# GpSimd's share of a sine in a top-k attention and cosine-gate kernel: reduced early in a slot only, with other chunk counts and another warm-up

## The chip, the cores and the metric

The kernel runs on one core of one Trainium2 chip. The metric is the device time of one execution in microseconds (us). Four executions of the kernel before took 1465.86, 1465.92, 1466.25 and 1466.51 us; their median is 1466.09 us.

## The reference

Inputs are `q`, `k`, `v` of shape (8, 8, 576, 64), `w_in` of shape (512, 2048) and `w_out` of shape (2048, 512). Cut to what matters:

```
scores = (1/8) * q @ k^T                       # per batch and head, 576 x 576
kth    = 32nd largest value of each row
attn   = softmax(where(scores >= kth, scores, -1e9))
x      = (attn @ v), heads side by side        # 4608 tokens x 512
h      = x @ w_in                              # 4608 x 2048
out    = (h * cos(h)) @ w_out                  # 4608 x 512
```

The weights arrive as 64-bit floats, and the kernel makes 32-bit ones of them itself ("decoding").

## The kernel before

**Units and slots.** A unit is 128 rows of queries (tokens) by one pair of heads. There are 36 blocks of 128 tokens and four pairs of heads, so 144 units; four units make a block of `x`. The program is one loop over slots, written out by hand, and the scheduler keeps that order on each engine: slot i looks for the top 32 values of unit i on VectorE, makes the exponentials of unit i-1 on ScalarE, sends unit i-2 out for its transpose, and in every even slot multiplies units i-4 and i-3 with `v` on TensorE. In this document slot i begins with VectorE's instruction at L255 (`rest`), the first of its search.

**One unit on its way.** TensorE makes the scores (L228) into two PSUM tiles, `sc` for columns 0 to 447 and a strip of `rim` for the rest. ScalarE copies them to SBUF (`take_scores`: L240 and L243; for unit 0 alone in three pieces, L242, L243, L245). VectorE folds the two halves of each row (L255, maximum), GpSimd adds and subtracts to get the minimum (L273, L282; in slots 7 to 11 VectorE takes the minimum itself, L263), and VectorE searches four times eight maxima in `rest` and two times eight in `low` (L360, L365). ScalarE masks (L389, L391) and exponentiates (L399). GpSimd splits the words into 16-bit halves (L432, L434), SyncE writes them to DRAM (`rows`, L442) and reads them back by a transposing DMA (`pT`, L448). TensorE multiplies with `v` (L485) into `rim`, and VectorE scales the result into `xT` (L494). As the values stand in the same bank as the strip of scores, ScalarE's L243 of an even slot comes behind L485, and L494 behind that.

**The second layer.** When all four units of a block are in `xT`, TensorE computes `h` in eight steps (`ff1`, L545), two of them to one of two PSUM banks `mm`, four of them to one tile `g` of 1024 columns. ScalarE empties a bank in two instructions (`take_first`, L559 and L561: a scaled copy `g` and a rounded copy `x`). Then GpSimd forms the argument of the sine, `g` minus the rounded number (`reduce_first` L581, `reduce_second` L590), ScalarE computes the sine (`sines`, L600, with a table load before it and another before the next L399), GpSimd multiplies (`gate`, L607), and TensorE computes `o` in eight steps of two columns of `w_out` each (`ff2`, L620). ScalarE empties `o` (L630) and writes it out. `feed` hands TensorE such steps at three places in each slot, and decides while the program is built, by counters: a tile that was reduced in a slot gets its sine in a later one, and `ff2` may use a gated tile two calls of `feed` after its gate (three in later slots). `w_out` may be used once `wq["ready"]` counts it.

**Weights.** 32 chunks of 512 KB, 16 of `w_in` and then 16 of `w_out`, are loaded by `load_weights(n, queue)` (L122) at the start of the slots: three before slot 0, then `n` in each slot, on SyncE's queue in slots 0 and 1 and on ScalarE's own queue after that. A chunk is decoded by ScalarE at the end of its slot (`decode_first`, L135 and L138), by VectorE after the third search of the next slot (L146) and by GpSimd right behind (L156), the chunk that came last first. A staging tile is shared with the tiles `g`, seven in all, and a load that finds none is left to the next slot.

**The order in a slot** of what the change touches:

```
load_weights(n, nc.sync if i < 2 else nc.scalar)
if x: send(x)
topk_first(u, w); fold_low(u); topk_round(u, 1); topk_round(u, 2)
decode_second(NP); decode_third()
...
feed(1); scores; values; sines; mask; take_banks(); exponentials; take_scores
topk_round(u, 3, both(w), z)
gate(1); feed(2); take_banks(); decode_first(NP)
reduce_first(); reduce_second()
feed(3)
```

Before the loop TensorE runs seven multiplications of a tile of ones (L813), the two head pairs of the first block are asked for, and unit 0's scores are made and taken.

Of the kernel before, what the change touches and what calls it, by code (L numbers as in the profile page):

```python
# [10 lines left out]
F32 = mybir.dt.float32  # L11
# [6 lines left out]
P = 128  # L18
# [12 lines left out]
def kernel(  # L31
# [9 lines left out]
    nc = tc.nc  # L41
# [6 lines left out]
    NP = H // 2  # L48
    NF = DF // P
    HS = S // 2  # L50
# [7 lines left out]
    small = ctx.enter_context(tc.tile_pool(name="small", bufs=4))  # L58
# [2 lines left out]
    ffw = ctx.enter_context(tc.tile_pool(name="ffw", bufs=2))  # L61

    ident = consts.tile([P, P], F32, tag="ident")
    ones = small.tile([P, P], F32, tag="ones", name="ones", bufs=1)
    nc.vector.memset(ones, 1.0)
    make_identity(nc, ident)
    halfpi = consts.tile([P, 1], F32, tag="halfpi")
    nc.vector.memset(halfpi, math.pi / 2.0)
# [26 lines left out]
        chunks.append((moe_w_out[f * P : (f + 1) * P, :], w))  # L95
    CHUNKS, XB = 7, 4
    BUSY = range(7, 12)
    ff = {"live": 0, "tick": 0, "now": 0, "credit": 0.0, "end": False, "kind": 0, "half": 0, "open": 0}

    wq = {"next": 0, "loaded": deque(), "second": deque(), "third": deque(), "done": 0, "ready": 0}  # L100

# [49 lines left out]
    def decode_third():  # L151

        while wq["third"]:
            st, w, _ = wq["third"].pop()
            wi = w.bitcast(I32)
            nc.gpsimd.tensor_tensor(out=wi, in0=wi, in1=st[:, :, 0], op=ALU.add)  # L156
            wq["done"] += 1
# [58 lines left out]
    SB = 448  # L216
# [18 lines left out]

    def take_scores(u):
        s = u["s"] = work.tile([P, 2, S], F32, tag="s", name="s", bufs=4)
        head = u["n"] == 0
        if not head:
            nc.scalar.copy(out=s[:, :, 0:SB], in_=u["sc"][:, :, 0:SB])  # L240
        else:
            nc.scalar.copy(out=s[:, :, HS:SB], in_=u["sc"][:, :, HS:SB])  # L242
        nc.scalar.copy(out=s[:, :, SB:S], in_=sc_ends[u["n"] % 2])  # L243
        if head:
            nc.scalar.copy(out=s[:, :, 0:HS], in_=u["sc"][:, :, 0:HS])  # L245
        if not u["folds"]:
            del u["sc"]

# [51 lines left out]
    def topk_first(u, w):  # L300

        u["top"] = tops[u["n"] % len(tops)]
        merges = w and w["folds"]
        if merges:
            merge_first(w)
        if u["folds"]:
            if u["n"] not in BUSY:
                fold_sum(u)
            fold_high(u)
        else:  # L310
            u["rest"] = work.tile([P, 2, S], F32, tag="rest", name="rest", bufs=1)
        if merges:
            merge_second(w)
        if u["folds"] and u["n"] in BUSY:
            fold_now(u)
        topk_round(u, 0, [lambda: bounds(w), lambda: distances(w)] if w else ())

    def topk_round(u, rnd, between=(), ahead=None):
        top, rest, lasts = u["top"], u["rest"], TOPK // 8 - 1
        end = TOPK - 1 - 8 * rnd  # L320
        at = top[:, :, end : end - 8 if rnd < lasts else None : -1, 0]
        if u["folds"]:
            search(
                at, rest[:, :, HS:S] if rnd == 0 else rest[:, :, 0:HS], rest[:, :, 0:HS], rnd < lasts,
                between if rnd < lasts else (),
            )
        else:
            search(at, u["s"] if rnd == 0 else rest, rest, rnd < lasts, between)
        if rnd < lasts:
            return  # L330
        del u["rest"]
        if u["folds"]:
            low = u.pop("low")
            for k in range(TOPK // 16):
                more = k < TOPK // 16 - 1
                if ahead and not more:
                    take_values(ahead)
                search(
                    top[:, :, 1 + 8 * k : 9 + 8 * k, 1], low, low, more,
                    () if more or rnd < lasts else between,  # L340
                )
# [3 lines left out]
    def merge_first(u):  # L345
        n = TOPK // 2 + 1
        u["lesser"] = u["top"].rearrange("p j r i -> p j (r i)")[:, :, 2 * n : 3 * n]
        nc.vector.tensor_reduce(
            out=u["lesser"], in_=u["top"][:, :, 0:n], axis=mybir.AxisListType.X, op=ALU.min
        )  # L350

    def merge_second(u):
        nc.vector.tensor_reduce(
            out=u["top"][:, :, TOPK - 1, 1], in_=u.pop("lesser"), axis=mybir.AxisListType.X,
            op=ALU.max,
        )
# [57 lines left out]
    def both(u):  # L414
        return [lambda: sums(u), lambda: reciprocal(u)] if u else ()
# [88 lines left out]
    for w in widths:  # L504
        blk = {"t0": t0, "w": w, "left": 0, "g": [], "gated": []}
# [12 lines left out]
    fresh = deque()  # L518
# [38 lines left out]
    def take_first(blk, g, x, mm, half):  # L557
        at = slice(half * 512, half * 512 + 512)
        nc.scalar.mul(out=g[:, at], in_=mm, mul=INV_2PI / UP)  # L559

        nc.scalar.activation(  # L561
            out=x[:, at].bitcast(I32), in_=mm, func=AF.Identity, bias=quarter, scale=INV_2PI / UP
        )
        if half == 1:
            fresh.append([blk, g, x, False])

    def take_banks():
        while full:
# [2 lines left out]

    def reduce_first():

        if not fresh:
            return
        _, g, x, _ = fresh[0]
        fresh[0][3] = True
        if ff["end"]:
            nc.vector.tensor_tensor(out=x, in0=g, in1=x.bitcast(I32), op=ALU.subtract)
            return  # L580
        nc.gpsimd.tensor_scalar(  # L581
            out=x, in0=x.bitcast(I32), scalar1=1.0, scalar2=0.0, op0=ALU.mult, op1=ALU.add
        )

    def reduce_second():
        if not fresh or not fresh[0][3]:
            return
        blk, g, x, _ = fresh.popleft()
        if not ff["end"]:
            nc.gpsimd.tensor_tensor(out=x, in0=g, in1=x, op=ALU.subtract)  # L590
        waiting.append((blk, g, x, ff["now"]))
# [104 lines left out]
    for n in range(NP, len(order)):  # L696
        i = last[order[n - 5]] if n >= 5 else 0
        load_at(max(i, 2 * NP + 2), load_qk, *order[n])
        i = last_values[order[n - 6]] if n >= 6 else 0
# [13 lines left out]
    def send(x):  # L713

        split(x)
        write_halves(x)
        transposes(x)

    def slot(i, u, w, x, z):
        n = 4 if i in (1, 2) else 3 if i < NP else 2  # L720
        if i < NP:
            for load, b, hp in at_once[i]:
                load(b, hp)
        load_weights(n, nc.sync if i < 2 else nc.scalar)
        if x:
            send(x)
        topk_first(u, w)
        fold_low(u)
        topk_round(u, 1)
        topk_round(u, 2)  # L730
        decode_second(NP)
        decode_third()
        made = scored.get(i, [])
        if z:
            take_banks()
        feed(1)

        for m in made:
            scores(m)
        if z:  # L740
            values(z)


        late = len(made) > 0

        decoding = i < 3 * NP
        if i % 2 or decoding:
            sines(1)
        if w:
            mask(w)  # L750
        take_banks()
        if w and late:
            exponentials(w)
        take_scores(units[i + 1])
        if w and not late:
            exponentials(w)
        topk_round(u, 3, both(w), z)
        if i in at_slot:
            load, b, hp = at_slot[i]
            load(b, hp)  # L760
        gate(1)
        feed(1 if len(made) == 2 else 2)
        take_banks()
        decode_first(NP)
        reduce_first()
        reduce_second()
        feed(1 if len(made) == 2 else 3)
        if i == LAST:
            sines(1)

    def last_slot(i, u, w, x, z):
        if u:
            topk_first(u, w)
            fold_low(u)
            topk_round(u, 1)
        else:
            bounds(w)
            distances(w)
        mask(w)
        exponentials(w)  # L780
        take_banks()
        sines(1)
        if z:
            values(z)
        if i + 1 < NU:
            scores(units[i + 1])
        if z:
            take_values(z)
        if i + 1 < NU:
            take_scores(units[i + 1])  # L790
        if x:
            send(x)
        if u:
            topk_round(u, 2, both(w))
            topk_round(u, 3)
        else:
            sums(w)
            reciprocal(w)
        normalise(w)
        gate(2)  # L800
        feed(2)
        transposes_now(w)
        take_banks()
        reduce_first()
        reduce_second()
        feed(1)
        values([w])
        take_values([w])
        feed(2)

    tt = ps.tile([P, 512], F32, tag="mm", name="warm", bufs=2)
    for _ in range(7):
        nc.tensor.matmul(tt[:, 0:P], ones, ones, start=True, stop=True)  # L813
    load_qk(0, 0)
    load_qk(0, 1)
    load_weights(3, nc.sync)
# [3 lines left out]
    for i in range(NU + 1):  # L820
# [4 lines left out]
        u, w = (units[i - n] if 0 <= i - n < NU else None for n in range(2))  # L825
        x = units[i - 2] if 0 <= i - 2 < LAST else None
# [52 lines left out]
```

## Time and profile before

| | |
|---|---|
| median of four executions | 1466.09 us |
| the profiled execution's own time | 1466.51 us |
| its span | 1464.7 us |
| mean granted clock of TensorE | 0.973 |
| busy: TensorE, VectorE, GpSimd, ScalarE | 1388.1, 1362.9, 1157.0, 1088.7 us |
| instructions | 30242 |

The span is the time from the first to the last instruction of the profiled execution, 1.8 us less than the execution's own time. A matrix multiplication of 32-bit floats leaves two records on TensorE, a transpose one. The profile's chain of waits follows the work that ended last back to the start; a line of the timeline shows start, busy time, engine, line and operands, and in brackets the idle time before it and what ended that.

### The profile page before, as it was taken

How to read it: one execution, taken by the hardware profiler on the slowest of the kernel's cores; microseconds unless marked ns; L12 is line 12 of the kernel's file. 1: busy time of each engine (PE TensorE's matmuls, PEld its weight loads, DVE VectorE, ACT ScalarE, POOL GpSimd, SP SyncE). 2: the span in 40 equal slices, each digit the busy share in tenths (PEclk: the TensorE clock that was granted, in tenths of full speed). 3: DMA queues.
4: the chain of work that ended last, by engine and by line, in shares of the span. 5: the costliest groups of instructions: out<-in, count | busy, mean ns of one | idle time of the engine just before them, and what ended most of it. 6: DMA issues, size and time to landing. Idle time of an engine off the chain costs nothing.

```text
span 1464.7 us, 30242 instructions
## 1 busy us (share of the span) xinstructions
PE 1388.1 (95%) x10290; PEld 1000.1 (68%) x10290; DVE 1362.9 (93%) x5214; ACT 1088.7 (74%) x1911; POOL 1157.0 (79%) x812
## 2 busy tenths in 40 slices
PE   4378899999999999999999999999999999999998
PEld 2165667777777777777777766777777776777675
DVE  7999899999999999999999999999999999999821
ACT  5777677777777777777777777777777777777641
POOL 5876788888888887888888888888888888888410
PEclk6589999999999999999999999999999999999999
DMA  8977576666665666657655666667665576655200
GB/s 264 278 216 206 151 187 173 159 168 175 192 151 152 152 197 171 166 152 187 190 159 149 151 183 180 170 148 183 192 173 144 144 176 167 163 148 151 62 8 15
DMA packets 427434, 240.00 MB, mean 164 GB/s; under 512 B 375952, under 2 KB 392592, under 8 KB 427280
## 3 DMA queue, kind: packets, MB, share of 16 engines
q1 hardware_dynamic: 418704, 216.88, 56.5%
q10 hardware_dynamic: 8576, 21.19, 4.3%
q8 instruction: 81, 1.33, 0.4%
q14 instruction: 73, 0.60, 0.1%
HBM read 45.09 MB, written 101.19 MB: 100 GB/s over the span
## 4 chain that ended last, share of the span: by engine, by line
PE 86%; DVE 5%; ACT 4%; DMA 3%; POOL 1%; issue 1%; SPq 0%; ACTq 0%; POOLq 0%
PE mm L545 33%; PE o L620 33%; PE rim L485 11%; PE sc L228 8%; DVE top L360 2%; PE rim L228 2%; DVE rest L365 1%; DMA st<-in_moe_w_in_dram 1%; ACT s L399 1%; ACT s L391 1%; DMA v<-in_v_dram 1%; DMA rows<-halves 1%; DMA pT<-rows 0%; ACT x L561 0%; ACT L600 0%
## 5 line engine op out<-in xcount | busy, mean ns | idle before, releaser
L545 PEld LDWEIGHTS mm<-xT,w_in 128*128 128x128 f32 x4608 | 541.4, 193 | 77.9 <-issue 64.6
L545 PE MATMUL mm<-xT,w_in 128*128 128x128 f32 x4608 | 544.8, 277 | 10.8 <-DVE xT L494 7.9
L620 PE MATMUL o<-w_out,g 128*128 128x512 f32 x1152 | 538.4, 601 | 8.6 <-POOL g L607 7.4
L360 DVE MAX8 top<-rest 128x8 f32<-128x288 f32 x1148 | 480.7, 454 | 0.0
L432 POOL COPY halves<-s 128x2304 uint16<-128x2304 uint16 x140 | 294.6, 2104 | 151.0 <-ACT s L399 149.7
L365 DVE MATCH_REPLACE8 rest<-top,rest 128x288 f32<-128x288 f32 (+1 forms) x860 | 377.1, 446 | 0.0
L620 PEld LDWEIGHTS o<-w_out,g 128*128 128x128 f32 x1152 | 203.0, 191 | 197.3 <-issue 186.5
L360 DVE MAX8 top<-low 128x8 f32<-128x288 f32 x568 | 239.9, 448 | 2.7 <-POOL low L282 2.7
L399 ACT ACTIVATE s<-s,nd 128x576 f32<-128x576 f32 x288 | 220.2, 767 | 0.8
L391 ACT ACTIVATE s<-s,top 128x576 f32<-128x576 f32 x288 | 206.1, 766 | 0.0
L282 POOL TENSOR_TENSOR low<-low,rest 128x576 int32<-128x576 int32 x137 | 193.5, 1412 | 10.7
L273 POOL TENSOR_TENSOR low<-s 128x576 int32<-128x576 int32 x137 | 193.4, 1412 | 5.7 <-ACT s L245 4.4
L228 PE MATMUL sc<-k,q 64*128 64x448 f32 (+1 forms) x640 | 154.2, 585 | 35.4 <-DMA k<-in_k_dram 15.0
L559 ACT ACTIVATE g<-mm 128x512 f32<-128x512 f32 x144 | 85.9, 596 | 130.1 <-PE mm L545 125.9
L590 POOL TENSOR_TENSOR x<-g,x 128x1024 f32<-128x1024 f32 x68 | 160.9, 2367 | 5.7
L485 PE MATMUL rim<-pT,v 128*64 128x128 f32 (+1 forms) x2560 | 159.4, 268 | 5.7 <-DMA pT<-rows 5.7
L607 POOL TENSOR_TENSOR g<-g,x 128x1024 f32<-128x1024 f32 x68 | 160.9, 2366 | 1.3 <-ACT x L600 1.3
L485 PEld LDWEIGHTS rim<-pT,v 128*64 128x64 f32 x2560 | 132.6, 139 | 16.0 <-issue 7.0
L240 ACT COPY s<-sc 128x896 f32<-128x896 f32 x143 | 128.4, 898 | 0.7 <-ACT ob L630 0.4
L243 ACT COPY s<-rim 128x256 f32<-128x256 f32 x144 | 55.1, 382 | 94.1 <-PE rim L485 94.1
L365 DVE MATCH_REPLACE8 low<-top,low 128x288 f32<-128x288 f32 x284 | 123.6, 443 | 0.0
L228 PEld LDWEIGHTS sc<-k,q 64*128 64x128 f32 (+1 forms) x640 | 46.4, 181 | 97.0 <-DVE rest L365 49.6
(62 smaller groups left out, 1334.6 us busy)
## 6 DMA issues: line engine op xcount, KB each, us to landing
rows<-halves SPq DMA_DIRECT2D x140, 640.0 KB, 3.0
out_dram<-ob ACTq DMA_DIRECT2D x36, 256.0 KB, 2.3
q<-in_q_dram SPq DMA_DIRECT2D x31, 288.0 KB, 3.6
v<-in_v_dram SPq DMA_DIRECT2D x32, 256.0 KB, 3.3
st<-in_moe_w_out_dram ACTq DMA_DIRECT2D x16, 512.0 KB, 4.5
st<-in_moe_w_in_dram SPq DMA_DIRECT2D x10, 512.0 KB, 6.6
k<-in_k_dram SPq DMA_DIRECT2D x31, 144.0 KB, 3.6
k<-in_k_dram SPq DMA_DIRECT2D x32, 128.0 KB, 3.6
```

The costliest lines, as they stand in the source:

```text
L228: nc.tensor.matmul(to[r0 : r0 + rows, j, 0 : k1 - k0], st["q"][d, q0 : q0 + rows], st["k"][d, k0:k1], start=True, stop=True,)
L273: nc.gpsimd.tensor_tensor(out=u["low"].bitcast(I32), in0=s[:, :, 0:HS], in1=s[:, :, HS:S], op=ALU.add)
L282: nc.gpsimd.tensor_tensor(out=low, in0=low, in1=u["rest"][:, :, HS:S].bitcast(I32), op=ALU.subtract)
L360: nc.vector.max(to[:, j], src[:, j])
L365: nc.vector.match_replace(rest[:, j], to[:, j], src[:, j], NEG)
L391: nc.scalar.activation(out=s[:, j], in_=s[:, j], func=AF.Prelu, bias=less[:, j, 1:2], scale=1.0, alpha=FAR)
L399: nc.scalar.activation(out=s[:, j], in_=s[:, j], func=AF.Exp, bias=nd[:, j : j + 1], scale=SCALE, accum_out=den[:, j, 0:1],)
L432: nc.gpsimd.tensor_copy(out=halves[:, :, 0 : 2 * S], in_=s.rearrange("p (k h) -> p h k", h=2))
L485: nc.tensor.matmul(o[d, to], lhsT, rhs, start=c == 0, stop=c == NT)
L545: nc.tensor.matmul(mm[:, at : at + w], w_in[f // FC][:, c, (f % FC) * P : (f % FC + 1) * P], blk["xT"][:, c], start=c == 0, stop=c == NC - 1,)
L590: nc.gpsimd.tensor_tensor(out=x, in0=g, in1=x, op=ALU.subtract)
L620: nc.tensor.matmul(o, g[:, at : at + P], w_out[f], start=f == 0, stop=f == NF - 1)
```

## The change

Four edits:

1. `reduce_first` and `reduce_second` are called at a second place too, right behind `decode_third()`. A new flag `ff["late"]` is set behind the fourth search of a slot and cleared at the start of the next. A tile whose second bank is emptied while the flag is set carries the number of that slot, and `reduce_first` leaves it until the next slot.
2. The chunk counts `n` of slots 0, 1, 2, ... were 3, 4, 4, 3, 2, 2, 2, ...; they are 3, 4, 3, 2, 2, 2, 2, 2, 3, 3, 3.
3. `take_scores` of unit 0 copies in two pieces as for every other unit.
4. The seven multiplications of a tile of ones, which VectorE had filled, become twelve transposes of the identity, which GpSimd makes; the tile of ones is gone.

```
-    ones = small.tile([P, P], F32, tag="ones", name="ones", bufs=1)
-    nc.vector.memset(ones, 1.0)
...
     def take_scores(u):
         s = u["s"] = work.tile([P, 2, S], F32, tag="s", name="s", bufs=4)
-        head = u["n"] == 0
-        if not head:
-            nc.scalar.copy(out=s[:, :, 0:SB], in_=u["sc"][:, :, 0:SB])
-        else:
-            nc.scalar.copy(out=s[:, :, HS:SB], in_=u["sc"][:, :, HS:SB])
+        nc.scalar.copy(out=s[:, :, 0:SB], in_=u["sc"][:, :, 0:SB])
         nc.scalar.copy(out=s[:, :, SB:S], in_=sc_ends[u["n"] % 2])
-        if head:
-            nc.scalar.copy(out=s[:, :, 0:HS], in_=u["sc"][:, :, 0:HS])
...
         if half == 1:
-            fresh.append([blk, g, x, False])
+            fresh.append([blk, g, x, False, ff["now"] if ff["late"] else 0])
...
     def reduce_first():
-        if not fresh:
+        if not fresh or (ff["late"] and not ff["end"] and fresh[0][4] == ff["now"]):
             return
...
     def slot(i, u, w, x, z):
-        n = 4 if i in (1, 2) else 3 if i < NP else 2
+        n = (3, 4, 3, 2)[i] if i < NP else 2 if i < 2 * NP else 3
...
+        ff["late"] = False
         topk_first(u, w)
         fold_low(u)
         topk_round(u, 1)
         topk_round(u, 2)
         decode_second(NP)
         decode_third()
+        reduce_first()
+        reduce_second()
...
         topk_round(u, 3, both(w), z)
+        ff["late"] = True
...
-    for _ in range(7):
-        nc.tensor.matmul(tt[:, 0:P], ones, ones, start=True, stop=True)
+    for _ in range(12):
+        nc.tensor.transpose(tt[:, 0:P], ident, ident)
```

`last_slot`, which runs for the last three units and the slot behind them, clears the flag at its start and reduces where it did.

More of the change, by code (lines that the diff above doesn't have):

```diff
@@ L97 @@
     BUSY = range(7, 12)
-    ff = {"live": 0, "tick": 0, "now": 0, "credit": 0.0, "end": False, "kind": 0, "half": 0, "open": 0}
+    ff = {"live": 0, "tick": 0, "now": 0, "credit": 0.0, "end": False, "kind": 0, "half": 0, "open": 0, "late": False}
     wq = {"next": 0, "loaded": deque(), "second": deque(), "third": deque(), "done": 0, "ready": 0}
@@ L572, in reduce_first @@
     def reduce_first():
-        if not fresh:
+        if not fresh or (ff["late"] and not ff["end"] and fresh[0][4] == ff["now"]):
             return
-        _, g, x, _ = fresh[0]
+        g, x = fresh[0][1:3]
         fresh[0][3] = True
@@ L587, in reduce_second @@
             return
-        blk, g, x, _ = fresh.popleft()
+        blk, g, x, *_ = fresh.popleft()
         if not ff["end"]:
@@ L771, in last_slot @@
     def last_slot(i, u, w, x, z):
+        ff["late"] = False
         if u:
```

## The prediction

> **What bounds the kernel now.** I read the chain of waits first, then TensorE's waits by stretch, then the timelines of the stretch that was left.
>
> ```profile
> PE 86%; DVE 5%; ACT 4%; DMA 3%; POOL 1%; issue 1%; SPq 0%; ACTq 0%; POOLq 0%
> ```
>
> TensorE (PE) is the chain. Asked for the stretch 185 to 1340 us, its waits are none at all. So the order of the two programs decides what can matter: from slot 16 on, every engine's instructions stand in the same order in both, the last slots too; only the chunk loads and decodings of slots 2 to 11, the order of a few steps of TensorE in slots 9 to 13, five reductions (slots 7, 8, 13 before; 8, 9, 14 after, two of them simply later) and the start differ. The end therefore moves by as much as the last moment at which TensorE still waits, and by what its clock does there. That moment is here:
>
> ```profile
> 166.44 0.61 PE L545 MATMUL mm<-xT,w_in 128*128 128x128 f32 x4
> 171.26 5.02 PE L545 MATMUL mm<-xT,w_in 128*128 128x128 f32 x28 [4.21 <-DVE xT L494]
> ```
>
> The 28 records behind it take 5.02 us where 28 of the usual pace (3.57 for 32) take 3.1: the granted clock there is 0.50 for 172 to 175 us. I call 171.26 the resumption. It is VectorE's xT of slot 14. VectorE's slots begin (L255) at 39.29 (slot 3), 50.47, 64.99, 74.65, 84.70, 95.00 (slot 8), 106.08, 117.84, 128.51, 138.80, 149.14, 160.17 (slot 14). The work is to move these.
>
> **Part 1: fewer early chunks.** The chain in slots 3 and 4:
>
> ```profile
> 45.24 8.12 DMA rows<-halves
> 53.38 7.17 DMA pT<-rows
> ...
> 60.68 1.97 PE L485 MATMUL rim<-pT,v 128*64 128x128 f32 x16 [4.79 <-DMA pT<-rows]
> ...
> 63.53 0.49 DVE L494 TENSOR_TENSOR xT<-rim,pT 128x128 f32<-128x128 f32 x2 [1.79 <-ACT s L243]
> ```
>
> Unit 1's `rows` take 8.12 us where 3.0 is the median, because three chunks were issued at 43.17 to 44.5 and the transposing read of unit 0 took SyncE's queue 7.89 us to issue (35.28 to 43.17), with four chunks in flight. The other such reads took 2.5 us without chunks and 4.4 to 5.1 with two, so about 1.3 per chunk. After: three chunks there, 1.3 off, so `rows` is issued at 43.9; two chunks beside it, so 512 KB less at the 420 GB/s of 48 to 52 us, 1.2 off. It lands at 50.7, 2.6 earlier, and `pT` at 57.9. TensorE then runs its 40 records partly at the full clock that it has at 56 to 59.6 us (1.3 instead of 2.4 us at best), so xT gains 2.7 to 3.8.
>
> Does VectorE get there? In slot 4 its L146 takes 3.00 us for two where 0.36 each is usual, while GpSimd runs L273 and L282 (55.89 to 58.83). GpSimd was held by L432 until the `rows` landed (53.36); now L156 has three chunks instead of four (1.25 less) and it is through at about 56, so L146 is nearly free, and one of three falls away (0.36). Slot 3 also begins 0.3 earlier (ScalarE issues one chunk less, 0.45 us on the chain at 34.66; VectorE was waiting 0.27) and has one L146 less. VectorE could be at L494 at 59.0. **Gain at slot 5: 3.4 us, from 2.4 (only the transfers' 2.6) to 4.5 (VectorE's own bound).** Slots 5 to 7 keep their lengths (9.66, 10.05, 10.30; no waits in them, two chunks as before). The chunks moved to slots 8 to 10 cost VectorE 0.36 in slots 9 and 11 and meet DMA shares of 0.6 to 0.85, so nothing else.
>
> **Part 2: the reductions of the first block.** Before:
>
> ```profile
> 104.65 2.38 POOL L607 TENSOR_TENSOR g<-g,x 128x1024 f32<-128x1024 f32 x1
> 106.98 1.07 POOL L581 TENSOR_SCALAR x<-x 128x1024 f32<-128x1024 int32 x1
> 108.13 2.36 POOL L590 TENSOR_TENSOR x<-g,x 128x1024 f32<-128x1024 f32 x1
> ...
> 113.50 2.54 POOL L156 TENSOR_TENSOR w_out<-w_out,st 128x512 int32<-128x512 int32 x2 [0.41 <-ACT s L391]
> 115.99 2.37 POOL L607 TENSOR_TENSOR g<-g,x 128x1024 f32<-128x1024 f32 x1
> ...
> 107.08 3.65 PE L620 MATMUL o<-w_out,g 128*128 128x512 f32 x4 [3.53 <-POOL g L607]
> ```
>
> The first tile is reduced at the end of slot 7, gets its sine in slot 8, and its gate ends at 107.03, 0.95 into slot 9; TensorE starts `o` then. After, that tile is emptied late in slot 7, so it is reduced in slot 8 behind L156; its sine stands in slot 9 and its gate at the end of slot 9, and on GpSimd's queue that is behind slot 9's three L156 and the second tile's reduction. TensorE's order still has eight columns of `o` (16 records) ahead of the scores of units 11 and 12, which slot 10's copies and values need. Counted from slot 9's L255: L146 at 6.28 (112.36 less 106.08), three in 1.09, 0.13 to GpSimd, three L156 3.7 (15.32 to 19.05), L581 1.13, L590 2.31, L607 2.37, TensorE 0.05 later: 17.1. The 16 records 8.8 (107.08 to 115.89, also from a cold clock), scores and values 4.5 (120.33 to 124.82), L243 and L494 0.5, to the next L255 1.43: slot 11 begins 32.3 after slot 9. Before it was 22.4. **Loss: 9.9 us.** TensorE idles some 19 us ahead of `o` instead of 3.53 and 2.53, and VectorE about 11 ahead of slot 10's L494. Behind the late gate on GpSimd's queue stands unit 8's split (L432), some 5 us later, and behind that its `rows` and `pT` on SyncE's; they are wanted in slot 12 only, 25 us on.
>
> Slot 8 loses its sine and two table loads (1.28 each) on ScalarE, so its L494 no longer waits 0.30: **gain 0.3**.
>
> **Part 3: slots 11 to 14.** Before, from slot 11 to the resumption: 42.75 us. In it VectorE waited 0.53 (slot 12) and 2.71 here, on its `low`:
>
> ```profile
> 160.58 1.04 POOL L581 TENSOR_SCALAR x<-x 128x1024 f32<-128x1024 int32 x1 [3.27 <-ACT x L561]
> ...
> 169.34 0.82 DVE L360 MAX8 top<-low 128x8 f32<-128x288 f32 x2 [2.71 <-POOL low L282]
> ```
>
> GpSimd stood 3.27 us at L581 of a bank emptied late, with the split and slot 14's L273 and L282 behind it. After, that reduction stands behind L282, which ends 2 us before VectorE asks. Slot 11 10.64 (10.29 and an L146), slot 12 9.81, slot 13 11.03 (its wait of 1.93 for the exponentials stays: ScalarE's sine is 1.1 sooner, but one more bank is emptied ahead of them, 1.15), and 8.38 in slot 14: 39.9. **Gain 2.9.** TensorE's own new waits there (GpSimd's L156 ahead of `o` in slot 12, about 2; a bank in slot 13, 2.4) lie under VectorE's slots; without that cover they would cost up to those amounts.
>
> **The clock at the resumption.** TensorE will have stood 1.8 us there instead of 4.21. Stalls of 1.26, 1.33 and 1.83 us (138.98, 157.36, 83.60) left the clock at 1.00, but one of 1.88 (127.41) was followed by 0.50. I take the warm case, 1.9 less 0.5 for unit 13's `pT`, which then comes late in slot 16: **gain 1.4**; the other bound is 0.
>
> The Trainium skill, "TensorE: Matmul & The Clock Gate", Part 1, says that the array goes cold only after about 3.4 us of idleness and warms after as much activity. By it the 1.8 us are safe and the gain is 1.4; the row at 127.41 speaks against it. The same rule speaks against the new warm-up, as twelve records are shorter than a window.
>
> **Part 4: the start**, costed at nothing. The 14 warm records (0.234 apart, from 1.05) become 12 (a transpose leaves one) from about 1.35, when GpSimd's identity is ready: scores of unit 0 at 4.2 instead of 4.33. If they ran at half clock they would take 2.3 (like 51.27 to 53.57) instead of 1.44. The copies are 0.1 shorter (0.79 and 0.37 for 1.25). All of it lies under slot 0's waits for the weights, 0.34 and 1.13 in VectorE's L146 (13.15, 14.71); without these it would cost at most 0.8.
>
> **Sum.** -3.4 - 0.3 + 9.9 - 2.9 - 1.4 = +1.9 us on the profiled execution's 1466.5, so 1468.4; that execution was 0.4 above the median, so 1468.0 us. About 0.2% (2.9 us) is what a measurement can tell from no change here; 1468.0 is inside it, close to its edge at 1469.0.
>
> **Rivals.** (a) Slower: the early relief is small. `rows` of unit 1 stays behind `v`, whose 512-byte pieces share the engines with the chunks, and `pT` still ends last in slot 4. With 1.0 instead of 3.4 the time is 1470.4; it decides below 2.4. For it: the shares of 0.95 and more at 46 to 52 us, which two chunks also fill. Against: the 1.3 us per chunk in the issue times. (b) Slower: slot 9's L146 collide with GpSimd as in slot 4 (2.2 us), or the resumption is cold (1.4): 1469.4 to 1471.6. Against: GpSimd should be free from 4.8 to 7.5 in slot 9. (c) Faster: the pause of Part 2 doesn't come, because I read the order wrong and `o` doesn't need that gate so early; then 9.9 goes and 1458 stays; it decides when TensorE's wait ahead of `o` is under 14 us. With half the pause, 1463.
>
> **How the numbers follow.** Forecast 0.46, (a) 0.24, (b) 0.17, (c) 0.13. Both (a) and (b) end over 1469.0: slower 0.41, same 0.46, faster 0.13. The forecast's own range is 1465 to 1469. The low end of the whole range, 1464.0: relief 4.5 (-1.1), slot 13's wait gone (-1.9), a warmer start of `o` (-1). The high end, 1472.0: relief 1.0 (+2.4) and a cold resumption (+1.4), rounded up.
>
> **What would show it.** Slot 5 begins near 61.6 and `pT` of unit 1 lands near 58; `rows` of unit 1 takes under 7 us; TensorE waits for the gate once, for 17 to 20 us, ending near 119.5; VectorE waits 10 to 12 us at slot 10's L494; no wait on `low` in slot 14; the resumption near 174.6, at full clock; no waits of TensorE from 190 to 1340. I am wrong if the wait for the gate is short, if slot 5 begins after 63, or if TensorE waits anew in the long stretch.

## The result and the profile after

| | before | after |
|---|---|---|
| median, runs | 1466.66 us, 68 | 1469.55 us, 43 |
| ratio of after to before, 95% interval | | 1.0024, 1.0017 to 1.0030 |
| the profiled execution's own time | 1466.51 us | 1467.65 us |
| its span | 1464.7 us | 1465.8 us |

The change makes the kernel 3.5 us slower by the ratio (2.5 to 4.4), 2.9 by the medians. That is just over the 0.2% that the prediction took as the limit of what can be told from no change. The profiled executions differ by 1.1 us only: before's lies at its median, after's 1.9 below its own. One execution each of e1 (1499.30 us) and of e3 (2762.67 us) below fell into a slower state and is left out of their ratios.

Line numbers are those of the kernel that ran. In after and the kernels built on its start they are 2 to 8 lower than in before: L255 is L247 there, L485 is L477, L494 is L486, L607 is L599, L620 is L612, L146 is L144.

The page's chain of waits of after, first line:

```profile
PE 82%; DVE 10%; ACT 4%; DMA 2%; SPq 1%; issue 1%; POOL 1%; ACTq 0%; POOLq 0%
```

VectorE's share has doubled and TensorE's is 4 points lower. TensorE's waits from 185 to 1340 us are 0.4 us in all, so the time is again made before slot 16. In nine profiled executions of kernels with and without parts of the change (before, after, e1 to e4, e9 to e11) the execution's time less the moment at which slot 16 begins lies between 1283.6 and 1285.2 us; in the other four, e5 to e8, which share a chip, between 1282.3 and 1282.5. So what the edits do they do by slot 16, and the 2 us behind it go with the chip.

The early slots of after, in the chain of waits by time (start, duration, what) and in VectorE's timeline:

```profile
42.31 6.60 DMA rows<-halves
48.93 6.46 DMA pT<-rows
...
59.82 0.75 DVE L247 TENSOR_TENSOR rest<-sc,s 128x576 f32<-128x576 f32 x1
```

Unit 1's `rows` take 6.60 us instead of 8.12, its `pT` lands at 55.4 instead of 60.6, and slot 5 begins at 59.82, 5.17 earlier.

The pause, in the timelines of GpSimd and TensorE:

```profile
108.01 3.77 POOL L154 TENSOR_TENSOR w_out<-w_out,st 128x512 int32<-128x512 int32 x3 [2.63 <-issue]
111.74 1.05 POOL L573 TENSOR_SCALAR x<-x 128x1024 f32<-128x1024 int32 x1
112.88 2.38 POOL L582 TENSOR_TENSOR x<-g,x 128x1024 f32<-128x1024 f32 x1
115.20 2.36 POOL L599 TENSOR_TENSOR g<-g,x 128x1024 f32<-128x1024 f32 x1
...
117.62 10.05 PE L612 MATMUL o<-w_out,g 128*128 128x512 f32 x16 [16.60 <-POOL g L599]
```

Slot 9 begins at 100.51, so TensorE starts `o` 17.1 us into it. Slots 9 and 10 take 33.54 us together. In the windows of the same stretch (length, then busy time and instructions of each engine, PEclk, DMA share, GB/s) the clock behind the pause is cold until about 124:

```profile
116.00:120.00 4.00, 2.38 (x3) 1.18 (x4) 4.00 (x18) 3.97 (x6) 3.95 (x3) 0.50 0.41 166
120.00:124.00 4.00, 4.00 (x6) 1.54 (x5) 3.53 (x13) 2.53 (x5) 2.62 (x3) 0.56 0.40 164
124.00:128.00 4.00, 4.00 (x11) 1.63 (x11) 0.00 (x0) 0.00 (x0) 4.00 (x2) 1.00 0.95 193
```

Slots 11 to 14 and the resumption, on TensorE:

```profile
171.76 0.61 PE L537 MATMUL mm<-xT,w_in 128*128 128x128 f32 x4
173.48 3.39 PE L537 MATMUL mm<-xT,w_in 128*128 128x128 f32 x28 [1.11 <-DVE xT L486]
```

The 28 records behind xT run at full clock, 3.39 us instead of 5.02, and VectorE no longer waits for `low`.

### The profile page after: what moved, and what is told of

It reads as the page before. It is cut to its first block, busy times and chain, and to the rows that moved or that the text cites. A ratio compares the mean times of both kernels' runs of the same rounds, so it can differ in the third digit from the quotient of the medians.

```text
span 1465.8 us, 30229 instructions
## 1 busy us (share of the span) xinstructions
PE 1389.2 (95%) x10288; PEld 999.1 (68%) x10288; DVE 1360.3 (93%) x5213; ACT 1088.0 (74%) x1910; POOL 1156.5 (79%) x812
## 4 chain that ended last, share of the span: by engine, by line
PE 82%; DVE 10%; ACT 4%; DMA 2%; SPq 1%; issue 1%; POOL 1%; ACTq 0%; POOLq 0%
PE o L612 31%; PE mm L537 30%; PE rim L477 10%; PE sc L226 7%; DVE top L352 4%; DVE rest L357 3%; PE rim L226 2%; DMA pT<-rows 1%; DMA rows<-halves 1%; DVE rest L247 1%; ACT s L391 1%; ACT L391 1%; DVE low L357 1%; DMA k<-in_k_dram 1%; ACT s L383 0%
## 5 line engine op out<-in xcount | busy, mean ns | idle before, releaser
L612 PE MATMUL o<-w_out,g 128*128 128x512 f32 x1152 | 539.5, 602 | 19.9 <-POOL g L599 16.6
L612 PEld LDWEIGHTS o<-w_out,g 128*128 128x128 f32 x1152 | 203.5, 191 | 209.3 <-issue 187.6
L226 PE MATMUL sc<-k,q 64*128 64x448 f32 (+1 forms) x640 | 157.2, 590 | 34.6 <-DVE rest L247 13.7
L477 PE MATMUL rim<-pT,v 128*64 128x128 f32 (+1 forms) x2560 | 160.4, 270 | 3.1 <-DMA pT<-rows 3.1
L599 POOL TENSOR_TENSOR g<-g,x 128x1024 f32<-128x1024 f32 x68 | 160.8, 2364 | 1.3 <-ACT x L592 1.3
L477 PEld LDWEIGHTS rim<-pT,v 128*64 128x64 f32 x2560 | 133.5, 139 | 13.2 <-issue 3.3
```

Of the source, the lines that this page charges most:

```text
L226: nc.tensor.matmul(to[r0 : r0 + rows, j, 0 : k1 - k0], st["q"][d, q0 : q0 + rows], st["k"][d, k0:k1], start=True, stop=True,)
L477: nc.tensor.matmul(o[d, to], lhsT, rhs, start=c == 0, stop=c == NT)
L612: nc.tensor.matmul(o, g[:, at : at + P], w_out[f], start=f == 0, stop=f == NF - 1)
```

## The experiments

All are compared with the kernel before, run beside them on the same chip; three groups share a chip each: e1 to e4 (before's median 1466.07), e5 to e8 (1468.30), e9 to e11 (1466.00). A comparison of ratios across groups also compares chips; no profile of before was taken beside e5 to e8. The ratio carries an interval of 0.1 to 0.2%; an amount in us is the ratio's distance from 1 times 1466. Single profiled executions scatter by up to some 5 us about their kernel's median, so a profile is used for its waits and the ratio for the time.

| | ratio, 95% interval | median | profiled |
|---|---|---|---|
| e1 chunk counts alone | 1.0019 (1.0004 to 1.0035) | 1469.20 | 1465.45 |
| e2 reductions alone | 1.0017 (1.0007 to 1.0027) | 1469.93 | 1469.03 |
| e3 start alone | 1.0001 (0.9987 to 1.0016) | 1466.10 | 1470.57 |
| e4 after, early reduction from slot 12 on only | 0.9993 (0.9975 to 1.0010) | 1464.87 | 1459.98 |
| e5 = e1 with one chunk moved from slot 10 to slot 7 | 0.9979 (0.9964 to 0.9994) | 1463.47 | 1462.12 |
| e6 = e4 with that chunk moved | 0.9957 (0.9942 to 0.9972) | 1461.95 | 1459.43 |
| e7 after, TensorE kept busy in the pause | 0.9989 (0.9979 to 0.9999) | 1466.48 | 1466.84 |
| e8 after, slot 9's gate ahead of the reduction | 0.9980 (0.9969 to 0.9991) | 1465.36 | 1464.22 |
| e9 after once more | 1.0023 (1.0012 to 1.0033) | 1469.68 | 1467.95 |
| e10 = e7 with more transposes | 1.0036 (1.0017 to 1.0054) | 1471.48 | 1476.56 |
| e11 late reductions alone | 0.9976 (0.9965 to 0.9987) | 1462.48 | 1465.62 |

**e1, the chunk counts alone.**

```
-        n = 4 if i in (1, 2) else 3 if i < NP else 2
+        n = (3, 4, 3, 2)[i] if i < NP else 2 if i < 2 * NP else 3
```

> The kernel before with the second edit alone (the other chunk counts). Theory (the trace of after shows slot 5 beginning 5.2 us earlier than before; fewer chunks beside unit 0's transposing read and unit 1's rows are the cause): slot 5 begins at 60 to 61 us, unit 1's rows take under 7 us, slot 4's two L146 take under 1 us, and the time is 4 to 5.5 us under before, near 1461.5 us, the resumption in slot 14 being earlier by as much. Rival 1 (the relief comes for the most part from the new start, by which the weights' transfers fall otherwise): slot 5 begins after 63 us and the time is within 1.5 us of before. Rival 2 (the chunks that arrive later cost as much in slots 8 to 11): slot 5 near 60 but the resumption unchanged at 171, time within 1.5 us of before.

Slot 5 begins at 59.16, as the theory has it, and still the kernel is 2.8 us slower (0.6 to 5.1). The theory's time fell, and rival 2 is the nearer one, though e1 is worse than it allowed. The profiled execution is 3.8 under its median and no slower than before's, so it can't show the 2.8; it shows where most of the relief goes, on TensorE in slots 8 and 9:

```profile
97.84 1.98 PE L485 MATMUL rim<-pT,v 128*64 128x128 f32 x16 [4.32 <-DMA pT<-rows]
...
115.20 2.08 PE L620 MATMUL o<-w_out,g 128*128 128x512 f32 x2 [5.96 <-POOL w_out L156]
```

The second line is a wait that neither before nor after has in these slots. `o`'s eighth column needs the eighth chunk of `w_out`, which now comes in slot 8 and is decoded by GpSimd in slot 9, behind the second tile's reduction (L156 three times, 111.38 to 115.14). With before's counts it was decoded in slot 8. The first line is unit 5's transposing read, which landed 12.8 us after its issue began, beside three loads; before's took 9.3 beside two. Slots 8 and 9 take 27.34 us instead of before's 22.84, so 4.5 of the 5.8 us by which slot 5 began earlier are gone by slot 10.

**e2, the reductions alone**: before with the first edit, old counts, old start.

```
+        ff["late"] = False
         topk_first(u, w)
...
         decode_third()
+        reduce_first()
+        reduce_second()
...
         topk_round(u, 3, both(w), z)
+        ff["late"] = True
```

> The kernel before with the first edit alone (the reductions). Theory (the gate of the first block's first tile comes a slot later and TensorE stands ahead of o): one wait of TensorE ahead of o of 14 to 18 us in slot 9, slot 9 to slot 11 10 to 11.5 us longer than before's 22.4, slots 11 to 14 shorter by 2 to 3 and the resumption warmer by up to 1.9: time 5 to 8 us over before, 1471 to 1474 us. If slot 9's unpredicted 1 us more (VectorE's wait of 2.97 at L399) is due to the third chunk of that slot, it is absent here, and the pause costs 10. Rival (the whole difference of after comes from elsewhere and the pause is absorbed): within 1.5 us of before.

```profile
119.97 9.96 PE L620 MATMUL o<-w_out,g 128*128 128x512 f32 x16 [18.77 <-POOL g L607]
```

The pause is there: 18.77 us once, slot 9 to slot 11 31.86, slot 14 9.38 instead of 12.20. With two chunks in slot 9 instead of three the gate ends 15.5 us after the slot's start instead of 17.1. The time, 2.5 us over before (1.0 to 4.0), is under the 5 to 8 expected: the mechanism holds and its price at the end is smaller than its price in slots 9 and 10. In the trace these two take 9.4 us more than before's, slots 11 to 15 give 4.6 of it back, and slot 9 had begun 1.6 earlier, so slot 16 begins 3.2 later. Besides, as e3 and e11 below show, executions with before's order have waits of their own in the same place.

**e3, the start alone**: twelve transposes and the uncut copies.

```
-    for _ in range(7):
-        nc.tensor.matmul(tt[:, 0:P], ones, ones, start=True, stop=True)
+    for _ in range(12):
+        nc.tensor.transpose(tt[:, 0:P], ident, ident)
```

> The kernel before with the third and fourth edits alone (the start). Theory (slot 0 begins 0.5 later since the twelve transposes leave the clock cold, all of it under VectorE's waits for the weights): within 0.7 us of before. Rival 1 (the new start moves the weights' transfers so that slot 1 begins 1.2 us earlier, as in the trace of after): 1 to 1.5 us under before. Rival 2 (the cold scores cost their time): 0.5 to 1 us over before.

The ratio is 1.0001: the start costs nothing, as predicted. Its profiled execution shows the scatter: slot 10 takes 13.96 us where before's took 10.67, with the same program there, by

```profile
128.45 1.97 PE L477 MATMUL rim<-pT,v 128*64 128x128 f32 x15 [3.69 <-DMA pT<-rows]
```

The same wait is 2.90 in e11 and 3.67 in e5. Slots 9 and 10 of kernels with before's order and counts there take 22.43 (before), 23.82 (e11) and 25.68 us (e3). Before's one profile, from which the prediction took 22.43, was the shortest of the three.

**e4, without the pause.**

```
-        reduce_first()
-        reduce_second()
+        if i >= 3 * NP:
+            reduce_first()
+            reduce_second()
...
-        ff["late"] = True
+        ff["late"] = i >= 3 * NP
```

> The changed kernel, with the early reduction and the flag from slot 12 on only; up to slot 11 a tile is reduced at the end of a slot as before. Theory (the relief of 5.2 us, the 2.9 us of slots 11 to 14 and the warmer clock add, and the pause is the only loss): no wait of TensorE ahead of o over 5 us in slots 8 to 11, slot 9 to slot 11 near 22.5, the resumption near 163 us, time 7 to 9.5 us under before, 1457 to 1459 us. Rival (the gains overlap: an earlier slot 5 makes later slots wait for something else, such as chunks of w_out or a free staging tile): 3 to 5 us under before.

TensorE's wait for the gate is gone (2.1 at most), but the time is 1.0 us under before (3.7 under to 1.5 over), not 7 to 9.5: the theory fell. TensorE waits for the same `w_out` instead, and slot 9 takes 12.70 us:

```profile
114.00 2.07 PE L612 MATMUL o<-w_out,g 128*128 128x512 f32 x2 [4.32 <-POOL w_out L154]
```

In after, the pause had covered this wait: it has none at `w_out` in slots 8 to 11. Against e9 (after once more, 1.0023, on another chip with nearly the same median of before) e4 is 4.4 us faster, and their intervals don't meet. So much of the time is the pause's.

**e5 and e6, one chunk a few slots earlier.** The counts of e1 and e4 with slot 10's third chunk asked for in slot 7 instead; TensorE's order is then before's.

```
-        n = (3, 4, 3, 2)[i] if i < NP else 2 if i < 2 * NP else 3
+        n = (3, 4, 3, 2, 2, 2, 2, 3, 3, 3, 2)[i] if i < 11 else 2
```

> The kernel before with the other chunk counts, but one chunk moved from slot 10 to slot 7 (3, 4, 3, 2, 2, 2, 2, 3, 3, 3, 2); TensorE's order is then before's, and GpSimd decodes the eighth chunk of w_out in slot 8 instead of slot 9. Theory (the gain of the early slots was given back in e1 by TensorE's 5.96 us at w_out in slot 9, and by the collision of unit 5's transposing read with three loads in slot 8): no wait at w_out over 1 us, slot 9 under 12.5 us instead of 14.36, time 2 to 5 us under before, 1461 to 1464 us. Rival (the waits for the transposing reads, not w_out, give it back): TensorE waits 3 us or more for pT in slots 6 to 10 and the time stays within 1.5 us of e1, 1467.5 to 1470.

> The kernel of e4 (other chunk counts, new start, flag and early reduction from slot 12 on) with the same chunk moved from slot 10 to slot 7, so that TensorE has before's order up to slot 11. Theory: e4's 4.32 us at w_out go, and the time is 3 to 4 us under e4, 1460.5 to 1462 us. Rival (the transposing reads decide): as e4, 1463.5 to 1466 us.

Neither profile has a wait at `w_out` in slots 8 to 11, so the moved chunk was its cause. e5 is 3.1 us under before (0.9 to 5.3) where e1 was 2.8 over, and e6 6.3 under (4.1 to 8.5) where e4 was 1.0 under. That these 5.9 and 5.3 us are the wait for `w_out` is not shown. From slot 5 to slot 16 the profiles differ by 0.7 us only (120.7 in e5, 121.4 in e1) and 0.6 (115.2 in e6, 115.9 in e4), as other waits stand in its place; e5 has the rival's mark in slot 10:

```profile
123.18 1.09 PE L485 MATMUL rim<-pT,v 128*64 128x128 f32 x16 [3.67 <-DMA pT<-rows]
```

And the chips differ: on that of e5 to e8 before's median is 2.2 higher, and the stretch behind slot 16, where the edits do nothing, is about 2 us shorter in all four profiles. If before has that shorter stretch too, it loses some 4 us more by slot 16 there than on the other chips; no profile shows where, or whether e1 and e4 would lose as much. e6's median is lower than before's in any of the groups, and by the ratios it is faster than both kernels.

**e7 and e10, the clock in the pause.** Transposes that nothing reads, on TensorE ahead of slot 9's `o`: 132 in e7, 172 in e10.

```
+        if i == 9:
+            busy = ps.tile([P, 512], F32, tag="mm", name="busy", bufs=2)
+            for _ in range(132):
+                nc.tensor.transpose(busy[:, 0:P], ident, ident)
```

> The changed kernel with 132 transposes of the identity on TensorE ahead of slot 9's o, to a bank that nothing reads; they fill the 16.6 us in which TensorE stood. Theory (of the pause's 11.1 us about 1.2 to 3 are the cold clock behind it): o's 16 records take 7 to 9 us instead of 10.05, and the scores and values behind them run at the full clock, so slot 9 to slot 11 is 30.5 to 32.5 instead of 33.54; time 1 to 3 us under the changed kernel's, 1466.5 to 1468.5. Rival (the clock behind the pause is not what VectorE waits for): within 0.5 us of the changed kernel, 1469 to 1470.

> As e7, with 172 transposes instead of 132, since e7's ended 5.18 us ahead of the gate and the clock was at 0.50 again behind that; 172 take about 19 us and end near the gate. Theory (the cold clock is the 1.25 us by which o's records, 10.05 to 10.18, exceed the 8.8 of before): TensorE stands under 2 us ahead of o, o's 16 records take 6.9 to 8.8, slot 9 to slot 11 is 30.3 to 32.3 instead of 33.5, time 1.5 to 3.2 us under e9. Rival (VectorE waits for something else there): slot 9 to 11 unchanged and the time within 0.7 us of e9.

e7's profile doesn't show what its time suggests. The transposes ended at 113.1, TensorE stood another 5.18 us, and `o` was as slow as in after (10.18):

```profile
118.28 10.18 PE L612 MATMUL o<-w_out,g 128*128 128x512 f32 x16 [5.18 <-POOL g L599]
```

Slots 9 and 10 took 33.71 us, so neither of the theory's marks came. Its median is 3.1 us under after's, at the edge of the theory's range, and by the ratios it is 5 under (before's median was 2.2 higher in this group than in the first). In the profiles its slot 16 begins 0.8 later than after's, and the stretch behind is 1.6 shorter, as in all four profiles of this chip. So the chip may be what makes it faster; after has no run on record beside it, and I leave that open. In e10's profile the transposes began at 109.83, 11.3 us later than in e7, and themselves became what `o` waited for, since the gate had ended at 126.1:

```profile
104.65 1.97 PE L477 MATMUL rim<-pT,v 128*64 128x128 f32 x16 [10.16 <-DMA pT<-rows]
...
109.83 18.94 PE L766 MATMUL busy<-ident 128*128 128x128 f32 x172
128.60 7.03 PE L612 MATMUL o<-w_out,g 128*128 128x512 f32 x16
```

A filling of fixed length holds `o` up whenever the work ahead of it is late, and e10 is 5.3 us slower than before (2.5 to 7.9), its slots 9 and 10 33.07 instead of 30.3 to 32.3; its time says nothing for the theory. But the last line gives the disputed price: at full clock the 16 records take 7.03 us. From `o`'s start to the start of slot 11 it is 13.43 us in e10, 15.45 in e9 (records 9.06), 16.43 in after (10.05) and 16.57 in e7 (10.18). Each step is that of the records, so VectorE waits for the cold clock to its full amount, 3.0 us in after.

**e8, the gate first.** After without the early reduction in slot 9 alone, so that GpSimd gates the first tile ahead of the second tile's reduction.

```
-        reduce_first()
-        reduce_second()
+        if i != 9:
+            reduce_first()
+            reduce_second()
```

> The changed kernel without the early reduction in slot 9 alone: there GpSimd multiplies the first tile's gate ahead of the second tile's reduction (3.5 us) instead of behind it; no other engine's order moves. Theory (TensorE's wait is GpSimd's queue in slot 9): TensorE's wait ahead of o 13 to 14 instead of 16.6, slot 9 to 11 about 30 instead of 33.54, time 3 to 3.5 us under the changed kernel, 1466 to 1466.6. Rival (the sine on ScalarE or the transposing reads end last there): less than 1 us, 1468.6 or more.

```profile
115.52 10.18 PE L612 MATMUL o<-w_out,g 128*128 128x512 f32 x16 [12.95 <-POOL g L599]
```

The wait is 12.95, the gate comes 13.6 us into slot 9 instead of 17.1, slots 9 and 10 take 30.21 us, and the profiled execution is 3.4 under after's. The theory holds for the wait: it is GpSimd's queue. What that is worth in time is less certain. The median is 4.2 under after's, where 3 to 3.5 were expected, but after did not run beside e8; it is 1.1 under that of e7, which ran beside it and whose slots 9 and 10 are 3.5 longer.

**e9, after once more.**

> The changed kernel itself once more, beside e10 and e11 on one chip. Theory (the loss of 3.5 us is the kernel's, and the difference of 1.1 between the two profiled executions was chance): 2 to 4.5 us over before; in the profile TensorE's wait ahead of o 15.5 to 18 and slot 9 to slot 11 33 to 34.5 us again, while the waits for pT in slots 4 to 8 may differ by 2 us. Rival (the chip's batch decides): within 1 us of before.

Ratio 1.0023, as the first time, and again the profiled execution lies 1.7 under the median. Slot 5 begins at 60.22. TensorE's wait ahead of `o` is 18.78 us, and slots 9 and 10 take 32.54 with `o`'s records at 9.06: the pause came again, the wait over and the slots just under what was expected. The loss in time is the kernel's in this group too, and not chance.

**e11, the late reductions alone**: before with the flag and the early reduction from slot 12 on, nothing else.

```
+        ff["late"] = False
         topk_first(u, w)
...
         decode_third()
+        if i >= 3 * NP:
+            reduce_first()
+            reduce_second()
...
         topk_round(u, 3, both(w), z)
+        ff["late"] = i >= 3 * NP
```

> The kernel before with the flag and the early reduction from slot 12 on, and nothing else: only GpSimd's order in slots 13 and 14 moves (the last tile's reduction goes behind slot 14's low). Theory (the prediction's slots 11 to 14 and the clock at the resumption): no wait on low in slot 14, slot 14 9.4 instead of 12.2, the resumption at full clock; time 3 to 4.5 us under before, ratio 0.997 to 0.998. Rival (the end is set by later waits, so a moment gained at slot 14 is lost again): within 1 us of before.

```profile
165.14 1.42 POOL L282 TENSOR_TENSOR low<-low,rest 128x576 int32<-128x576 int32 x1
166.53 1.05 POOL L581 TENSOR_SCALAR x<-x 128x1024 f32<-128x1024 int32 x1
...
170.18 3.39 PE L545 MATMUL mm<-xT,w_in 128*128 128x128 f32 x28 [1.39 <-DVE xT L494]
```

The reduction stands behind `low`, slot 14 takes 9.38, the resumption is at full clock, and the kernel is 3.5 us faster than before (1.9 to 5.1). e5's ratio times e11's is 0.9955; e6, which has both and the new start, has 0.9957. Within their intervals these parts add.

## Why the prediction was right, and where it was not

The predicted time, 1468.0, is 1.6 under the median and its range holds it. The ratio lies just beyond the prediction's own edge at 1469.0, where it had put rivals (a) and (b). That the time came out so near is in part luck: the relief of Part 1 was 1.8 us larger than forecast and the loss of Part 2 1.2 larger, and they work against each other.

**What TensorE's early waits decide**: right. Slot 16's start sets the time within 1.6 us in nine profiles and within 0.2 in the four of e5 to e8.

**Part 1, the early relief**: the mechanism was right and the size too small. Predicted 3.4, with 4.5 as bound; after shows 5.17. Of this 1.16 is already there when slot 1 begins. e1 and e2 have 0.9 of it with the old start, and e9 has none with the new one (18.39 against before's 18.34), so it goes with the execution and not with the start. Over the nine profiles with the new counts slot 5 begins at 60.0 on average (59.1 to 61.9), over the four with the old ones at 64.9 (63.8 to 66.0): 4.9 us. Mis-sized was the transfers' gain, 2.6 us from 1.3 per chunk in the issue times: the transposing read of unit 0 took 5.52 us to issue beside three chunks (5.02 in e9), 2.4 less than before's 7.89, `rows` went out at 42.31 instead of the 43.9 expected, and `pT` landed 5.2 us earlier. VectorE then waits 0.58 us at slot 4's `xT`, its two L144 take 0.87, and slot 4 itself takes 10.84 us instead of 14.52.

The step that failed is the sentence behind it, that the chunks moved to slots 8 to 10 cost VectorE 0.36 here and there "so nothing else". It weighed DMA shares and not who needs the chunk that is moved: e1 and e4 show 5.96 and 4.32 us of TensorE's waiting for it, and e5 and e6 show both gone with one chunk moved back. What the wait costs in time is open (e5 and e6 above). The forecast did not have to pay for it, because after has the pause in the same place, which covers this wait.

**Part 2, the pause**: right in place and cause. The gate ended where the count of GpSimd's queue put it, 17.1 us into slot 9, and TensorE waited once, 16.6 us in after and 18.8 in e9 (17 to 20 predicted), and VectorE 9.06 and 8.89 at slot 10's `xT` (10 to 12 predicted). The loss in the trace was 11.1 and 10.1 us instead of 9.9: the records of `o` had been taken at 8.8, from before's row, and took 10.05 and 9.06 from a colder clock. VectorE's wait of 2.97 us for the exponentials in slot 9 (after's L399, before's L407) was not foreseen either, but e7 has none of it and takes as long (33.71), so it lay under the pause. What the prediction lacked was that before's 22.43 us for slots 9 and 10 isn't a fixed number: against the mean of the three profiles with before's order and counts (24.0: before, e3 and e11) the two of after lose 9.1.

**Part 3 and the resumption**: right. Slots 11 to 14 and the rest up to the resumption took 39.43 us (39.9 predicted), the resumption was warm behind 1.11 us of standing, and e11 alone gives 3.5 where 2.9 and 1.4 were predicted.

**Part 4, the start**: right at nothing. The scores of unit 0 ran cold, 2.44 us for 1.44, as the prediction's other case had it; e3 shows no cost.

**From the profile to the median**: predicted as 0.4 between the profiled execution and the median, which was before's. In the profiles the sum came to +1.1 and +1.4 us (1467.65 and 1467.95 against 1466.51), close to the +1.9 predicted; both of after's profiled executions lie 1.7 to 1.9 under their kernel's median, and that is where the other half of the loss comes from. e10's profile shows what such a later execution can look like, with unit 5's `pT` late by 10.16 us in slot 8 in code that it shares with after. That this makes after's upper half is possible, but not shown: the timed runs have no trace.

**The rivals**: (a) came about in its size, not by its way; the relief came in full and the time was as if a good part of it hadn't. (b) did not: no L144 of slot 9 was slowed as in before's slot 4, and the resumption was warm. (c) did not: the pause came.

## What to carry to other kernels

Where a load is moved to a later slot, follow it to the instruction that first needs it, through every engine that prepares it and behind everything that stands ahead of it on those queues; the DMA's load says little. Two losses at the same place need not add: a wait that lies under a pause can come out once the pause is mended, so each part has to be tried alone and with the others. Parts that are to be compared belong on the same chip. And a single profile gives one execution's waits for its DMAs; where the terms of a sum are a few us, take them from several profiles.

## What the runs showed of the hardware

**A transposing read's landing.** Unit 5's `pT`, issued at the end of slot 7 beside slot 8's three loads of 512 KB, landed 9.8 us after the start of its issue in after, 6.8 in e9, 12.8 in e1 and 17.7 in e10; in before, beside two loads, 9.3. In e10 the DMA engines were busy and moved little; the windows of e10, with the DMA share and GB/s last:

```profile
94.00:98.00 4.00, 0.50 (x10) 0.26 (x6) 4.00 (x16) 2.37 (x6) 0.69 (x1) 1.00 1.18 76
98.00:102.00 4.00, 0.00 (x0) 0.00 (x0) 1.47 (x6) 0.00 (x0) 3.92 (x4) 0.60 1.29 81
```

Why it is one time 6.8 and another 17.7 us is open. The Trainium skill, "Advanced Engine Details and Errata", section "X-Bar Transpose (TRN2)", expects 350 to 400 GB/s of transposing transfers, as fast as plain ones; the 76 and 81 GB/s at a full DMA share in e10 are far from it.

**The clock behind a pause.** The granted clock was 0.50 behind 5.18, 12.95, 16.60 and 18.78 us of standing alike, and the 16 records then took 10.18, 10.18, 10.05 and 9.06 us instead of 7.03. At half speed that is a cold stretch of 4.1 to 6.3 us, in no order by the length of the pause. The Trainium skill, "TensorE: Matmul & The Clock Gate", Part 1, gives about 3.4 us of sustained work until the clock is released; by it the records would lose half of that, an estimate of 1.7 us, and these lost 2.0 to 3.2. Standing for 1.11 and 1.39 us (after, e11) left the clock at full speed. So did 1.96 us in e6 (ahead of 126.25), while 2.46 us in e1 (ahead of 169.61) and before's 1.88 were followed by 0.50: the length of one short stop does not settle it.
